# Longer runs for Q and K, score groups of two pairs, and a copy that puts K^T back in token order, in an attention-into-MoE kernel on one core

## The chip, the core and the metric

The kernel runs on one core of a Trainium2 chip. The metric is the device time of one launch in microseconds; lower is better. Before the change it takes 311.21 us (median of 3 runs, 310.49 to 313.24). Executions of one kernel differ: these three by 0.9%. Runs are compared inside one job, on the same chip, with runs of the kernel before that the job shares. A ratio below is the mean time of one kernel's fast runs over that of the other's fast runs of the same rounds, so it is not quite the ratio of the medians quoted beside it. The profile shows one execution in microseconds from its start. Its engines are PE (TensorE, matmuls), ACT (ScalarE), DVE (VectorE), POOL (GpSimd) and SP (SyncE, which here issues most transfers). PSUM is the memory that TensorE writes its results to.

## The reference

Sliding-window causal attention (8 batches, 8 heads, 576 tokens, 64 columns a head, window 64), whose output goes straight into a two-layer MoE-style product:

```python
scores = scale * np.matmul(q, k.transpose(0, 1, 3, 2))      # q, k, v: (8, 8, 576, 64)
mask = (rel >= 0) & (rel < 64)
attn = softmax(where(mask, scores, -1e9))
x = (attn @ v).transpose(0, 2, 1, 3).reshape(4608, 512)     # tokens by features
h = x @ w_in                                                # (512, 2048)
out = (h * clip(h + 3, 0, 6) / 6) @ w_out                   # (2048, 512)
```

## The kernel before

A Python planner holds an estimated clock for each engine and emits instructions in the order that its estimates give. The hardware then runs each engine's list in that order, and waits where data is missing (DVE's lines below show it).

The 4608 tokens are cut into nine steps of 512. A step T has a *first product* (x times w_in, 64 matmuls of 512 columns, eight chunks; ACT makes relu, DVE makes `gT`) and a *second product* (gT times w_out, 64 matmuls). Into the second product of step T the attention of batch T+1 is inserted at fixed places. For batches 2 to 7:

```python
def tr(t, i=i, n=n):                 # i = 0: Q, 1: K
    def fn(s):
        nc.sync.dma_start_transpose(out=QK_tiles[b % NQT][:, i * NG : (i + 1) * NG, :]..., in_=n[:]...)
        fr, land = moved(s, 655, 230)          # the plan's KB and GB/s
        ...
        return land
...
def moved(now, kb, rate):
    dma["t"] = max(dma["t"], now) + kb / rate
    land = dma["t"] + 1.9 + dma["lag"]         # lag is 0.8 once the weights are loaded
    return max(now + 0.06, dma["t"] - 5.0), land
...
# loads of Q, K: 128 tokens at a time, 64 floats (256 bytes) a run
in_=src[b, :, kb * P : kb * P + ss, :].rearrange("h s d -> s h d")
...
# first product: three PSUM tiles are shared by all chunks
hT = two_banks([("g", T, c)])                  # free again when gT of the chunk is made
nc.tensor.matmul(hT[:, j, dst : dst + w], lhsT=win16[...], rhs=xT[:, g, src : src + w], ...)
...
REST = ((4, "S", 0), (10, "S", 1), (17, "S", 2), (17, "PV", 0), (23, "S", 3), (23, "PV", 1),
        (28, "PV", 2), (33, "PV", 3))          # after which of the 64 products what is inserted
```

Q and K are loaded naturally, cast to bf16 on Pool, and transposed by DMA into one single buffer `QKT`. S is the score matmuls of a pair of heads with its exponentials on ACT and its mask on DVE, PV is P times V.

The softmax here doesn't subtract the row's maximum and nothing guards it: scores larger than these inputs give would overflow.

Of the kernel before, what the change touches and what calls it, by code (L numbers as in the profile page):

```python
# [10 lines left out]
F32 = mybir.dt.float32  # L11
# [3 lines left out]
MULT = mybir.AluOpType.mult  # L15
# [6 lines left out]
NQT = 1  # L22
NPT = 4
VGAP = 1.8
VGAP2 = 1.8
# [79 lines left out]
def kernel(  # L105
# [15 lines left out]
    assert D == 64 and NG * P == DM and WINDOW == D  # L121
    KB = (S + P - 1) // P
    SP = KB * P
    R = 9
# [71 lines left out]
    NV = NG * KB * 2 * VW  # L196
    W_ring = [runs_flat[:, i * NV : (i + 1) * NV].rearrange("p (g k h w) -> p g k h w", g=NG, k=KB, h=2) for i in range(2)]
    BL = S // D

# [20 lines left out]
    def band(t, fill):  # L220
# [24 lines left out]
        out=m64[:], in_=m64[:], pattern=[[-1, D]], compare_op=ISGE, fill=0.0, base=-1, channel_multiplier=1), "m64")  # L245
    pl.op("DVE", 26.2, 0.1, lambda s: nc.vector.tensor_copy(out=mask64[:], in_=m64[:]) and None, "mask64", deps=("m64",))
    for i, t in enumerate(W_ring):
# [24 lines left out]
    def cast_op(eng, out_ap, in_ap):  # L272
# [7 lines left out]
        "cast": lambda e, n: {"POOL": 0.18, "DVE": 0.19, "ACT": 0.18}[e] + {"POOL": 0.83e-3, "DVE": 0.45e-3, "ACT": 0.83e-3}[e] * n,  # L280
        "spread": lambda e, n: {"DVE": 0.156, "ACT": 0.165}[e] + {"DVE": 1.04e-3, "ACT": 0.83e-3}[e] * n,
        "x": lambda e, n: {"DVE": 0.156, "ACT": 0.165}[e] + {"DVE": 0.52e-3, "ACT": 0.83e-3}[e] * n,
    }

    def copy_op(kind, engs, n, ready, out_ap, in_ap, key, then=None):

        cost = {e: COST[kind](e, n) for e in engs}
        if len(cost) == 1:
            eng = engs[0]
            pl.op(eng, ready, cost[eng], cast_op(eng, out_ap, in_ap), key, then)  # L290
        else:
            pl.op(cost, ready, 0, lambda eng: cast_op(eng, out_ap, in_ap), key, then)

# [129 lines left out]
    def load_nat(b):  # L423
        for i, src in enumerate((q, k)):
# [7 lines left out]
            def tr(t, i=i, n=n):  # L432
                def fn(s):
                    nc.sync.dma_start_transpose(
                        out=QK_tiles[b % NQT][:, i * NG : (i + 1) * NG, :].rearrange("d g (k t) -> d (g k) t", t=P),
                        in_=n[:].rearrange("p g k d -> p (g k d)"),
                    )
                    fr, land = moved(s, 655, 230)
                    pl.free["SP"] = fr
                    pl.mark(("issued", b, i), s)  # L440
                    return land
                d = (("S", b - NQT, NG - 1),) if b >= NQT else ()
                if b > 2:
                    d += (("s1", b - 1),)
                pl.op("SP", t, 0.1, fn, ("tr", b, i), deps=d)
            for kb in range(KB):
                ss = min(P, S - kb * P)
                def go(s, i=i, src=src, kb=kb, ss=ss, T=T, n=n, tr=tr):
                    if kb == 0:
# [9 lines left out]
                    fr, land = moved(s, 262 * ss / P, 205)  # L459
                    def done(t):  # L460
                        T["left"] -= 1
                        if not T["left"]:
                            tr(t)
                    pl.op("POOL", land, 0.61,
# [162 lines left out]
    def kwin(b, g, i, h):  # L627

        t = QK_tiles[b % NQT]
        c = (2 * g + 1 if b < NR6 else NG + g) * SP + (i - 1) * D  # L630
        return t[:].rearrange("p a s -> p (a s)")[h * D : (h + 1) * D, c : c + P]

    def blocks(b, g):
        n = b * NG + g
        return P_ring[n % NPT][:].rearrange("p h k w -> p (h k w)")[:, 0 : 2 * S].rearrange("p (h c) -> p h c", h=2)

    def scores64(b, g):

        for i in range(2):
            pl.wait(("tr", b, i))  # L640
        QT, pT = qk(b, 0, g), blocks(b, g)
        for part in range(2):
            i0, i1 = ((0, 5), (5, BL))[part]
            st = two_banks([("exp", b, g, part)])
            for i in range(i0, i1):
                for h in range(2):
                    c = (i - i0) * D
                    nc.tensor.matmul(  # L648
                        st[:, h, c : c + D], lhsT=kwin(b, g, i, h), rhs=QT[h * D : (h + 1) * D, i * D : (i + 1) * D],
                        start=True, stop=True,  # L650
                    )
            pl.pe((0.25, 0.22)[part])
            def ex(s, st=st, i0=i0, i1=i1):
                nc.scalar.activation(  # L654
                    out=pT[:, :, i0 * D : i1 * D], in_=st[:, :, 0 : (i1 - i0) * D], func=EXP, scale=scale,
                )
            def msk(t):
                pl.op("DVE", t, 0.8, lambda s: nc.vector.tensor_tensor(  # L658
                    out=pT.rearrange("p h (i w) -> p (h i) w", w=D), in0=pT.rearrange("p h (i w) -> p (h i) w", w=D),
                    in1=mask64[:].unsqueeze(1).to_broadcast([P, 2 * BL, D]), op=MULT,  # L660
                ) and None, ("mask", b, g), deps=("mask64",))
            pl.op("ACT", pl.t + 0.1, (0.8, 0.69)[part], ex, ("exp", b, g, part), msk if part else None)
        pl.mark(("S", b, g), pl.t)

    def pv64(b, g, o):

        V, W, pT = V_ring[b % 2], W_ring[b % 2], blocks(b, g)
        for h in range(2):
# [64 lines left out]
    def xt(b, g, cell):  # L733
# [9 lines left out]
        x0 = x_at(b)  # L743
        copy_op("x", X_ENG[b][g], S, pl.t + 0.1, xT[:, g, x0 : x0 + S], tr[:, 0:S], ("x", b, g))


    def s1(T):
# [11 lines left out]
        for c in range(NCH):  # L759
# [4 lines left out]
            if c == 0:  # L764
                order.sort(key=lambda x: x[2] == NG - 1 and x[1] is parts[-1])
            for j, (dst, src, w), g in order:
                nc.tensor.matmul(  # L767
                    hT[:, j, dst : dst + w], lhsT=win16[:, g, (2 * c + j) * P : (2 * c + j + 1) * P],
                    rhs=xT[:, g, src : src + w], start=(g == 0), stop=(g == NG - 1),
                )  # L770
                pl.pe(0.216 * w / TB)
# [53 lines left out]
    def finish(T, ts, acc, c0, c1):  # L825
        u0 = T * TB + ts * P
        nst = T * 4 + ts + (c0 > 0)
        cell = {}
        def cp(s):
# [3 lines left out]
            if c0:  # L833
                nc.scalar.dma_start(out=out[u0 : u0 + P, c0:c1], in_=osb[:, c0:c1])
        def store(t):
            def fn(s):
                nc.sync.dma_start(out=out[u0 : u0 + P, c0:c1], in_=cell["o"][:, c0:c1])
                fr, land = moved(s, 262, 375)
                pl.free["SP"] = fr
                return land  # L840
            pl.op("SP", t, 0.1, fn, ("st", nst))
# [29 lines left out]
    for r in held.pop():  # L871
# [6 lines left out]
             (0, "X", 1), (0, "PV", 3), (0, "X", 2), (0, "X", 3))  # L878
    REST = ((4, "S", 0), (10, "S", 1), (17, "S", 2), (17, "PV", 0), (23, "S", 3), (23, "PV", 1),
            (28, "PV", 2), (33, "PV", 3))  # L880
    for T in range(NTB):
# [40 lines left out]
```

## Time and profile before

| | before |
|---|---|
| median, us | 311.21 (310.49 to 313.24) |
| span of the profiled run, us | 308.9 |
| TensorE busy | 96% |
| DVE, ACT, Pool busy | 52%, 51%, 38% |
| DMA packets | 153,487 |

The costliest groups of TensorE, from the page. The columns are line, engine, operation, output and inputs, form and count, then busy microseconds and mean nanoseconds of one, then idle microseconds just before them and what ended them:

```profile
L815 PE MATMUL acc<-wout,gT 128*128 128x512 bf16 (+2 forms) x559 | 129.3, 373 | 3.1 <-issue 2.2
L767 PE MATMUL ps<-xT,win 128*128 128x512 bf16 (+4 forms) x696 | 125.8, 340 | 0.5
...
L648 PE MATMUL ps<-QKT 64*128 64x64 bf16 x432 | 10.5, 191 | 1.5 <-DMA QKT<-nat 1.2
```

The means are latencies of overlapped matmuls, so 129.3 and 125.8 are not independent costs. Before all 696 recorded matmuls of the first product (L767) TensorE was idle for 0.5 us together.

### The profile page before, as it was taken

How to read it: one execution, taken by the hardware profiler on the slowest of the kernel's cores; microseconds unless marked ns; L12 is line 12 of the kernel's file. 1: busy time of each engine (PE TensorE's matmuls, PEld its weight loads, DVE VectorE, ACT ScalarE, POOL GpSimd, SP SyncE). 2: the span in 40 equal slices, each digit the busy share in tenths (PEclk: the TensorE clock that was granted, in tenths of full speed). 3: DMA queues.
4: the chain of work that ended last, by engine and by line, in shares of the span. 5: the costliest groups of instructions: out<-in, count | busy, mean ns of one | idle time of the engine just before them, and what ended most of it. 6: DMA issues, size and time to landing. Idle time of an engine off the chain costs nothing.

```text
span 308.9 us, 6664 instructions
## 1 busy us (share of the span) xinstructions
PE 296.3 (96%) x2746; PEld 153.7 (50%) x2787; DVE 161.5 (52%) x208; ACT 157.4 (51%) x199; POOL 118.1 (38%) x185
## 2 busy tenths in 40 slices
PE   8979999998999999999999999999999999999995
PEld 3544445643544454875444544454665544444443
DVE  5576675566614673377437742674276516404610
ACT  5946677465515661567156724662367246315611
POOL 3267558537824751457228522762252000000000
PEclk9999999999999999999999999999999999999999
DMA  8999999999999997999799989999990520010011
GB/s 225 255 361 388 388 324 213 268 223 222 202 191 262 252 221 152 214 232 202 168 221 260 200 165 209 258 214 164 218 188 33 118 74 0 34 70 35 0 68 70
DMA packets 153487, 58.38 MB, mean 189 GB/s; under 512 B 142064, under 2 KB 143344, under 8 KB 153456
## 3 DMA queue, kind: packets, MB, share of 16 engines
q1 hardware_dynamic: 125184, 50.80, 75.8%
q10 hardware_dynamic: 28272, 7.15, 12.3%
q8 instruction: 22, 0.36, 0.5%
q14 instruction: 9, 0.07, 0.1%
HBM read 36.70 MB, written 9.44 MB: 149 GB/s over the span
## 4 chain that ended last, share of the span: by engine, by line
PE 74%; DMA 14%; SPq 6%; POOL 4%; issue 2%; ACT 0%; ACTq 0%; POOLq 0%
PE acc L815 35%; PE ps L767 32%; DMA st<-in_v_dram 5%; DMA st<-in_moe_w_out_dram 5%; PE ps L672 3%; PE ps L648 3%; SPq L354 2%; DMA st<-in_q_dram 2%; SPq L329 2%; DMA xT<-opg 1%; SPq L412 1%; POOL V L277 1%; POOL runs L277 1%; POOL wout L277 1%; PE ps L737 0%
## 5 line engine op out<-in xcount | busy, mean ns | idle before, releaser
L779 DVE SCALAR_TENSOR_TENSOR gT<-t,ps 128x1024 bf16<-128x1024 bf16 x72 | 87.8, 1221 | 100.9 <-ACT t L776 100.9
L815 PE MATMUL acc<-wout,gT 128*128 128x512 bf16 (+2 forms) x559 | 129.3, 373 | 3.1 <-issue 2.2
L767 PE MATMUL ps<-xT,win 128*128 128x512 bf16 (+4 forms) x696 | 125.8, 340 | 0.5
L776 ACT ACTIVATE t<-ps,half 128x1024 bf16<-128x1024 f32 x72 | 80.1, 1114 | 48.9 <-PE ps L767 48.9
L767 PEld LDWEIGHTS <-win 128*128 128x128 bf16 x704 | 65.2, 98 | 59.8 <-issue 0.4
L815 PEld LDWEIGHTS <-gT 128*128 128x128 bf16 x592 | 53.6, 98 | 57.9
L832 ACT COPY osb<-acc 128x512 f32<-128x512 f32 (+2 forms) x37 | 21.3, 576 | 76.0 <-PE acc L815 75.3
L277 POOL CAST runs<-st 64x512 bf16<-64x512 f32 (+1 forms) x49 | 31.1, 635 | 65.2 <-DMA st<-in_v_dram 41.3
L277 POOL CAST nat<-st 128x512 bf16<-128x512 f32 x48 | 33.8, 716 | 20.2 <-DMA st<-in_k_dram 13.4
L654 ACT ACTIVATE pT<-ps 128x640 bf16<-128x640 f32 (+1 forms) x48 | 28.7, 650 | 11.2 <-PE ps L648 11.1
L713 DVE TENSOR_TENSOR opg<-ps,rec 128x640 bf16<-128x640 f32 x32 | 26.4, 824 | 1.1
L658 DVE TENSOR_TENSOR pT<-pT,mask 128x1152 bf16<-128x1152 bf16 x24 | 20.2, 843 | 6.9 <-ACT pT L654 6.9
L277 POOL CAST V<-st 128x512 bf16<-128x512 f32 (+1 forms) x30 | 19.3, 643 | 3.8 <-DMA st<-in_v_dram 2.2
L648 PEld LDWEIGHTS <-QKT 64*128 64x128 bf16 x432 | 7.6, 95 | 11.4 <-issue 9.7
L602 ACT ACTIVATE pT<-ps 128x768 bf16<-128x768 f32 x16 | 12.7, 834 | 0.8 <-PE ps L593 0.7
L672 PE MATMUL ps<-runs,pT 128*64 128x65 bf16 x288 | 12.4, 197 | 0.2 <-POOL runs L277 0.2
L672 PEld LDWEIGHTS <-pT 128*64 128x64 bf16 x480 | 9.6, 111 | 6.0 <-issue 4.1
L710 DVE RECIPROCAL rec<-ps 128x10 f32<-128x10 f32 x32 | 6.9, 217 | 9.8 <-PE ps L672 8.4
L648 PE MATMUL ps<-QKT 64*128 64x64 bf16 x432 | 10.5, 191 | 1.5 <-DMA QKT<-nat 1.2
L672 PE MATMUL ps<-V,pT 128*64 128x65 bf16 x192 | 11.5, 198 | 0.0
L276 ACT COPY QKT<-ps 128x1152 bf16<-128x1152 bf16 x8 | 8.9, 1129 | 4.8 <-PE ps L562 4.8
L274 DVE CAST runs<-st 128x576 bf16<-128x576 f32 x14 | 7.2, 520 | 5.8 <-DMA st<-in_q_dram 3.9
(60 smaller groups left out, 118.9 us busy)
## 6 DMA issues: line engine op xcount, KB each, us to landing
out_dram<-osb SPq DMA_DIRECT2D x35, 256.0 KB, 3.7
st<-in_q_dram SPq DMA_DIRECT2D x24, 256.0 KB, 6.0
st<-in_k_dram SPq DMA_DIRECT2D x24, 256.0 KB, 5.4
st<-in_v_dram ACTq DMA_DIRECT2D x24, 256.0 KB, 5.1
st<-in_moe_w_out_dram SPq DMA_DIRECT2D x4, 1024.0 KB, 13.1
st<-in_moe_w_in_dram SPq DMA_DIRECT2D x3, 1024.0 KB, 10.3
st<-in_q_dram SPq DMA_DIRECT2D x8, 288.0 KB, 6.7
st<-in_k_dram SPq DMA_DIRECT2D x8, 288.0 KB, 6.3
```

The source lines that it names most:

```text
L277: return lambda s: nc.gpsimd.tensor_copy(out=out_ap, in_=in_ap) and None
L602: nc.scalar.activation(out=pT[:, :, kbs[0] : kbs[0] + 2, 0:QW], in_=st[:, :, 0 : 2 * QW].rearrange("p h (k w) -> p h k w", k=2), func=EXP, ...
L648: nc.tensor.matmul(st[:, h, c : c + D], lhsT=kwin(b, g, i, h), rhs=QT[h * D : (h + 1) * D, i * D : (i + 1) * D], start=True, stop=True,)
L654: nc.scalar.activation(out=pT[:, :, i0 * D : i1 * D], in_=st[:, :, 0 : (i1 - i0) * D], func=EXP, scale=scale,)
L658: pl.op("DVE", t, 0.8, lambda s: nc.vector.tensor_tensor(out=pT.rearrange("p h (i w) -> p (h i) w", w=D), in0=pT.rearrange("p h (i w) -> p ...
L672: nc.tensor.matmul(o[odd * D : (odd + 1) * D, h, m * VW : (m + 1) * VW], lhsT=pT[:, h, i * D : (i + 1) * D], rhs=(V if i % 2 else W)[:, g, ...
L713: nc.vector.tensor_tensor(out=opg[:].rearrange("p k h d -> p h k d"), in0=ov[:, :, :, 0:D], in1=rec[:].unsqueeze(3).to_broadcast([P, 2, KB ...
L767: nc.tensor.matmul(hT[:, j, dst : dst + w], lhsT=win16[:, g, (2 * c + j) * P : (2 * c + j + 1) * P], rhs=xT[:, g, src : src + w], start=(g ...
L776: nc.scalar.activation(out=t1[:], in_=hT[:], func=RELU, bias=half[:], scale=1.0 / 6.0)
L779: nc.vector.scalar_tensor_tensor(out=gT[:, 2 * c : 2 * c + 2, :], in0=cell["t"][:], scalar=1.0, in1=hT[:], op0=MIN, op1=MULT,)
L815: nc.tensor.matmul(accs[ts][:, c0:c1], lhsT=gT[:, fc, ts * P : (ts + 1) * P], rhs=wout16[:, fc, c0:c1], start=(fc == 0), stop=(fc == NFC - 1),
L832: nc.scalar.copy(out=osb[:, c0:c1], in_=acc[:, c0:c1])
```

## The change

Its intent is to take work off the DMA, the switches and the PSUM tiles. Four consecutive tokens lie together in memory, 4 x 64 floats. If partition p takes tokens 4p to 4p+3, a run is 1 KB instead of 256 bytes. The transposed Q and K then stand in the order (token mod 4, token div 4). For Q this order is carried on: scores read Q in blocks of 4 x 16 columns, the mask and the first product follow, and the store writes every fourth row. K must be in token order for the sliding window, so five copies per batch straighten it into a tile `KN`; each goes to whichever of Pool and DVE the plan expects to finish it sooner. Scores go in groups of two pairs, in three parts of six blocks of 64 queries. Their places in the second product move later.

```diff
+LONG = (0, 1)
+KN_ENG = ("POOL", "DVE")
...
+        "kn": lambda e, n: {"DVE": 0.12, "POOL": 0.2}[e] + {"DVE": 1.2e-3, "POOL": 1.65e-3}[e] * n,
...
-                pl.op("SP", t, 0.1, fn, ("tr", b, i), deps=d)
+                pl.op("SP", t, 0.1, fn, ("tr", b, i), straighten if i else None, deps=d)
+            def straighten(t):
...
+                kd = (("S", b - 1, NG - 1), "knz")
+                copy_op("kn", KN_ENG, NG * D, t, KN[:, :, D + J * P : D + S], Kp[:, :, J * P : S], None, one, deps=kd)
+                for g in range(NG):
+                    copy_op("kn", KN_ENG, J * P, t, KN[:, g, D : D + J * P].rearrange("d (p j) -> d p j", j=J),
+                            Kp[:, g, 0 : J * P].rearrange("d (j p) -> d p j", j=J), None, one, deps=kd)
...
+                            in_=src[b, 4 * hh : 4 * hh + 4, 0 : J * P, :].rearrange("h (p j) d -> p h (j d)", j=J),
...
+        pl.wait(("tr", b, 0))
+        pl.wait(("kn", b))
...
+                if T >= NR6:
+                    i0, i1 = dst // D, (dst + w) // D
+                    xs = xs.rearrange("d (i j p) -> d j i p", j=J, p=D // J)
+                    hs = hT[:, j].rearrange("f (j i p) -> f j i p", j=J, p=D // J)[:, :, i0:i1]
...
+        rows = rows.rearrange("(p j) d -> j p d", j=J)[ts] if T >= NR6 else rows[ts * P : (ts + 1) * P]
...
-    REST = ((4, "S", 0), (10, "S", 1), (17, "S", 2), (17, "PV", 0), (23, "S", 3), (23, "PV", 1),
-            (28, "PV", 2), (33, "PV", 3))
+    REST = ((11, "S", 0), (18, "S", 1), (25, "PV", 0), (25, "PV", 1), (35, "PV", 2), (35, "PV", 3))
```

More of the change, by code (lines that the diff above doesn't have):

```diff
@@ L122 @@
     KB = (S + P - 1) // P
+    J = S // P
     SP = KB * P
@@ L197 @@
     W_ring = [runs_flat[:, i * NV : (i + 1) * NV].rearrange("p (g k h w) -> p g k h w", g=NG, k=KB, h=2) for i in range(2)]
+    KN = runs_flat[:, 2 * NV : 2 * NV + NG * (D + S)].rearrange("p (g t) -> p g t", g=NG)
     BL = S // D
@@ L245 @@
         out=m64[:], in_=m64[:], pattern=[[-1, D]], compare_op=ISGE, fill=0.0, base=-1, channel_multiplier=1), "m64")
-    pl.op("DVE", 26.2, 0.1, lambda s: nc.vector.tensor_copy(out=mask64[:], in_=m64[:]) and None, "mask64", deps=("m64",))
+    pl.op("DVE", 26.2, 0.1, lambda s: nc.vector.tensor_copy(
+        out=mask64[:].rearrange("k (j p) -> k j p", j=J), in_=m64[:].rearrange("k (p j) -> k j p", j=J)) and None, "mask64", deps=("m64",))
+    pl.op("DVE", 0.0, 0.2, lambda s: nc.vector.memset(KN[:, :, 0:D], 0.0) and None, "knz", deps=(("T", NR6 - 1, NG - 1),))
     for i, t in enumerate(W_ring):
@@ L281, with copy_op @@
         "spread": lambda e, n: {"DVE": 0.156, "ACT": 0.165}[e] + {"DVE": 1.04e-3, "ACT": 0.83e-3}[e] * n,
+        "kn": lambda e, n: {"DVE": 0.12, "POOL": 0.2}[e] + {"DVE": 1.2e-3, "POOL": 1.65e-3}[e] * n,
         "x": lambda e, n: {"DVE": 0.156, "ACT": 0.165}[e] + {"DVE": 0.52e-3, "ACT": 0.83e-3}[e] * n,
     }
-    def copy_op(kind, engs, n, ready, out_ap, in_ap, key, then=None):
+    def copy_op(kind, engs, n, ready, out_ap, in_ap, key, then=None, deps=()):
         cost = {e: COST[kind](e, n) for e in engs}
@@ L289, in copy_op @@
             eng = engs[0]
-            pl.op(eng, ready, cost[eng], cast_op(eng, out_ap, in_ap), key, then)
+            pl.op(eng, ready, cost[eng], cast_op(eng, out_ap, in_ap), key, then, deps=deps)
         else:
-            pl.op(cost, ready, 0, lambda eng: cast_op(eng, out_ap, in_ap), key, then)
+            pl.op(cost, ready, 0, lambda eng: cast_op(eng, out_ap, in_ap), key, then, deps=deps)
     def load_items():
@@ L444, in tr, with one, done, go @@
                     d += (("s1", b - 1),)
-                pl.op("SP", t, 0.1, fn, ("tr", b, i), deps=d)
-            for kb in range(KB):
+                pl.op("SP", t, 0.1, fn, ("tr", b, i), straighten if i else None, deps=d)
+            def straighten(t):
+                Kp = QK_tiles[b % NQT][:, NG : 2 * NG, :]
+                left = [NG + 1]
+                def one(t):
+                    left[0] -= 1
+                    if not left[0]:
+                        pl.mark(("kn", b), t)
+                kd = (("S", b - 1, NG - 1), "knz")
[3 more added lines that the diff above has]
+                            Kp[:, g, 0 : J * P].rearrange("d (j p) -> d p j", j=J), None, one, deps=kd)
+            def done(t, T=T, tr=tr):
+                T["left"] -= 1
+                if not T["left"]:
+                    tr(t)
+            if i in LONG:
+                for hh in range(2):
+                    def go(s, i=i, src=src, hh=hh, T=T, n=n, done=done):
+                        if hh == 0:
+                            T["t"] = stage.tile([P, H, J * D], F32, name="st", tag="st")
+                        nc.sync.dma_start(
+                            out=T["t"][:, 4 * hh : 4 * hh + 4, :],
+                            in_=src[b, 4 * hh : 4 * hh + 4, 0 : J * P, :].rearrange("h (p j) d -> p h (j d)", j=J),
+                        )
+                        fr, land = moved(s, 524, 320)
+                        for g in (2 * hh, 2 * hh + 1):
+                            pl.op("POOL", land, 0.62, cast_op(
+                                "POOL", n[:, g, 0:J, :].rearrange("p j (h d) -> p h j d", h=2),
+                                T["t"][:, 2 * g : 2 * g + 2, :].rearrange("p h (j d) -> p h j d", j=J)),
+                                ("cast", b, i, g), done)
+                        return fr
+                    yield b, deps, go
+            for kb in (KB - 1,) if i in LONG else range(KB):
                 ss = min(P, S - kb * P)
-                def go(s, i=i, src=src, kb=kb, ss=ss, T=T, n=n, tr=tr):
+                def go(s, i=i, src=src, kb=kb, ss=ss, T=T, n=n, done=done):
                     if kb == 0:
@@ L459, in go @@
                     fr, land = moved(s, 262 * ss / P, 205)
-                    def done(t):
-                        T["left"] -= 1
-                        if not T["left"]:
-                            tr(t)
                     pl.op("POOL", land, 0.61,
@@ L627, in kwin @@
     def kwin(b, g, i, h):
-        t = QK_tiles[b % NQT]
-        c = (2 * g + 1 if b < NR6 else NG + g) * SP + (i - 1) * D
-        return t[:].rearrange("p a s -> p (a s)")[h * D : (h + 1) * D, c : c + P]
-    def blocks(b, g):
-        n = b * NG + g
-        return P_ring[n % NPT][:].rearrange("p h k w -> p (h k w)")[:, 0 : 2 * S].rearrange("p (h c) -> p h c", h=2)
-    def scores64(b, g):
-        for i in range(2):
-            pl.wait(("tr", b, i))
-        QT, pT = qk(b, 0, g), blocks(b, g)
-        for part in range(2):
-            i0, i1 = ((0, 5), (5, BL))[part]
-            st = two_banks([("exp", b, g, part)])
-            for i in range(i0, i1):
+        return KN[h * D : (h + 1) * D, g, i * D : i * D + P]
@@ new lines, with turned, scores64 @@
+    halves = {}
+    NB = 6
+    def turned(t, i):
+        if i == BL - 1:
+            return t[:, i * D : (i + 1) * D].rearrange("d (p j) -> d j p", j=J)
+        return t[:, 0 : J * P].rearrange("d (j p) -> d j p", j=J)[:, :, i * (D // J) : (i + 1) * (D // J)]
+    def scores64(b, gg):
+        pl.wait(("tr", b, 0))
+        pl.wait(("kn", b))
+        pT = P_ring[(b * 2 + gg) % NPT][:].rearrange("p h k w -> p (h k w)")[:, 0 : 4 * S].rearrange("p (h c) -> p h c", h=2)
+        todo = [(2 * gg + a, i) for a in range(2) for i in range(BL)]
+        for part in range(3):
+            st = two_banks([("exp", b, gg, part)])
+            for c, (g, i) in enumerate(todo[part * NB : part * NB + NB]):
@@ L646, in scores64 @@
                 for h in range(2):
-                    c = (i - i0) * D
                     nc.tensor.matmul(
-                        st[:, h, c : c + D], lhsT=kwin(b, g, i, h), rhs=QT[h * D : (h + 1) * D, i * D : (i + 1) * D],
-                        start=True, stop=True,
-                    )
-            pl.pe((0.25, 0.22)[part])
-            def ex(s, st=st, i0=i0, i1=i1):
+                        st[:, h, c * D : (c + 1) * D], lhsT=kwin(b, g, i, h),
+                        rhs=turned(qk(b, 0, g), i)[h * D : (h + 1) * D], start=True, stop=True,
+                    )
@@ L654, in ex, with msk @@
+            pl.pe(0.27)
+            def ex(s, st=st, part=part):
                 nc.scalar.activation(
-                    out=pT[:, :, i0 * D : i1 * D], in_=st[:, :, 0 : (i1 - i0) * D], func=EXP, scale=scale,
+                    out=pT[:, :, part * NB * D : (part + 1) * NB * D], in_=st[:, :, 0 : NB * D], func=EXP, scale=scale,
                 )
-            def msk(t):
+            def msk(t, a=part - 1):
+                P_half = pT[:, :, a * S : (a + 1) * S].rearrange("p h (i w) -> p h i w", w=D)
@@ L658, in msk @@
                 pl.op("DVE", t, 0.8, lambda s: nc.vector.tensor_tensor(
-                    out=pT.rearrange("p h (i w) -> p (h i) w", w=D), in0=pT.rearrange("p h (i w) -> p (h i) w", w=D),
-                    in1=mask64[:].unsqueeze(1).to_broadcast([P, 2 * BL, D]), op=MULT,
-                ) and None, ("mask", b, g), deps=("mask64",))
-            pl.op("ACT", pl.t + 0.1, (0.8, 0.69)[part], ex, ("exp", b, g, part), msk if part else None)
-        pl.mark(("S", b, g), pl.t)
+                    out=P_half, in0=P_half,
@@ L665, in pv64 @@
+                    in1=mask64[:].unsqueeze(1).unsqueeze(1).to_broadcast([P, 2, BL, D]), op=MULT,
+                ) and None, ("mask", b, 2 * gg + a), deps=("mask64",))
+            pl.op("ACT", pl.t + 0.1, 0.82, ex, ("exp", b, gg, part), msk if part else None)
+        for a in range(2):
+            halves[b, 2 * gg + a] = pT[:, :, a * S : (a + 1) * S]
+            pl.mark(("S", b, 2 * gg + a), pl.t)
     def pv64(b, g, o):
-        V, W, pT = V_ring[b % 2], W_ring[b % 2], blocks(b, g)
+        V, W, pT = V_ring[b % 2], W_ring[b % 2], halves.pop((b, g))
@@ L743, in xt, with one @@
         x0 = x_at(b)
-        copy_op("x", X_ENG[b][g], S, pl.t + 0.1, xT[:, g, x0 : x0 + S], tr[:, 0:S], ("x", b, g))
+        if b == 0:
+            copy_op("x", X_ENG[b][g], S, pl.t + 0.1, xT[:, g, x0 : x0 + S], tr[:, 0:S], ("x", b, g))
+            return
+        c = NR6 * TB - b * S
+        left = [2]
+        def one(t):
+            left[0] -= 1
+            if not left[0]:
+                pl.mark(("x", b, g), t)
+        copy_op("x", X_ENG[b][g], c, pl.t + 0.1, xT[:, g, x0 : x0 + c], tr[:, 0:c], None, one)
+        copy_op("x", X_ENG[b][g], S - c, pl.t + 0.1,
+                xT[:, g, x0 + c : x0 + S].rearrange("d (i j p) -> d i j p", j=J, p=D // J),
+                tr[:, c:S].rearrange("d (i p j) -> d i j p", j=J, p=D // J), None, one)
     def s1(T):
@@ L766, in s1 @@
             for j, (dst, src, w), g in order:
+                xs, hs = xT[:, g, src : src + w], hT[:, j, dst : dst + w]
+                if T >= NR6:
+                    i0, i1 = dst // D, (dst + w) // D
+                    xs = xs.rearrange("d (i j p) -> d j i p", j=J, p=D // J)
+                    hs = hT[:, j].rearrange("f (j i p) -> f j i p", j=J, p=D // J)[:, :, i0:i1]
                 nc.tensor.matmul(
-                    hT[:, j, dst : dst + w], lhsT=win16[:, g, (2 * c + j) * P : (2 * c + j + 1) * P],
-                    rhs=xT[:, g, src : src + w], start=(g == 0), stop=(g == NG - 1),
+                    hs, lhsT=win16[:, g, (2 * c + j) * P : (2 * c + j + 1) * P],
+                    rhs=xs, start=(g == 0), stop=(g == NG - 1),
                 )
@@ L825, in finish @@
     def finish(T, ts, acc, c0, c1):
-        u0 = T * TB + ts * P
+        rows = out[T * TB : (T + 1) * TB]
+        rows = rows.rearrange("(p j) d -> j p d", j=J)[ts] if T >= NR6 else rows[ts * P : (ts + 1) * P]
         nst = T * 4 + ts + (c0 > 0)
@@ L833, in cp @@
             if c0:
-                nc.scalar.dma_start(out=out[u0 : u0 + P, c0:c1], in_=osb[:, c0:c1])
+                nc.scalar.dma_start(out=rows[:, c0:c1], in_=osb[:, c0:c1])
         def store(t):
             def fn(s):
-                nc.sync.dma_start(out=out[u0 : u0 + P, c0:c1], in_=cell["o"][:, c0:c1])
+                nc.sync.dma_start(out=rows[:, c0:c1], in_=cell["o"][:, c0:c1])
                 fr, land = moved(s, 262, 375)
```

## The prediction

> **What bounds the kernel now.** I read the page's first parts, then the chain that ended last, then TensorE's own waits, then one steady batch in order of time. The page first:
>
> ```profile
> PE 296.3 (96%) x2746; PEld 153.7 (50%) x2787; DVE 161.5 (52%) x208; ACT 157.4 (51%) x199; POOL 118.1 (38%) x185
> ...
> DMA  8999999999999997999799989999990520010011
> ...
> DMA packets 153487, 58.38 MB, mean 189 GB/s; under 512 B 142064, under 2 KB 143344, under 8 KB 153456
> ```
>
> The DMA row is full for three quarters of the span and nearly every packet is under 512 B, which invites the reading "DMA-bound". TensorE at 96% contradicts it. The chain decides; this is the stretch of the second MoE product that carries batch 3's attention:
>
> ```profile
> 106.53 0.86 PE acc L815 x4
> 107.39 0.37 PE ps L648 x18
> 107.76 1.40 PE acc L815 x6
> ...
> 111.14 0.37 PE ps L648 x18
> 111.51 0.44 PE ps L672 x20
> 111.95 1.18 PE acc L815 x5
> 113.14 0.15 issue
> ...
> 124.20 0.82 PE ps L767 x8
> ```
>
> It is TensorE after TensorE: scores (L648), P times V (L672) and MoE products (L815, L767), no transfer and no other engine. From 90 us on the only other pieces are short "issue" ones. What TensorE waited for, in the whole run:
>
> ```profile
> PE acc L815 <- issue: 2.2, 14, 0.2
> PE ps L850 <- DVE idle L202: 1.3, 1, 1.3
> PE ps L648 <- DMA QKT<-nat: 1.2, 1, 1.2
> PE ps L737 <- DVE opg L713: 1.1, 2, 0.6
> ```
>
> One transfer wait, 1.2 us: the scores of batch 2 start at 75.17 because the transposed K of that batch lands then. So the shortening of Q and K loads has 1.2 us to remove; everything else that DMA does is already beside TensorE.
>
> One steady step, from 106.5 to 124.2, takes 17.67 us. 64 products of 512 columns at 215.7 ns are 13.80; 4 x 0.37 of scores and 4 x 0.44 of P times V are 3.24. What is left, 0.63 us, goes to six switches from MoE work to attention and back, 0.10 each; three show as "issue" of 0.15 to 0.16.
>
> **The Trainium skill.** "TensorE: Matmul & The Clock Gate", section "Wait — 56ns, not 53.3ns?", gives 215.7 ns from start to start at 512 columns. The trace agrees: the first MoE product of this step runs from 92.28 to 106.36, 14.08 us for 64, or 220 ns with its beginning. There is nothing to win inside the products.
>
> "SBUF — State Buffer", section "Door 1: The DMA port swizzle", has a note that reads at full rate need at least two hits in each 16-byte line, and that scattered PSUM patterns slow matmuls. The new moving operands run 16 bf16 (32 bytes) before they jump, whole lines, the odd tail block steps 8 bytes, two hits a line, and the PSUM output is written in runs of 16 floats. By that page neither the scores nor the MoE products slow down. No matmul of the kernel before reads like this, so the trace can't confirm it.
>
> "DMA: Bandwidth & Descriptors", section "Specifications", puts the line-rate minimum at 512 B. The trace agrees in kind: the stretch of the 1024-KB weight loads reaches 388 GB/s in the page's GB/s row, the stretches of 256-byte runs show 150 to 270 under the same full DMA row. So 1-KB runs will be much cheaper for the DMA.
>
> "GPSIMD Engine Reference", section "Performance pitfalls for Q7 kernels", charges about 2.9 cycles an element when the read step is over 8 bytes. The straightening copy reads with a step of 256 bytes. 512 elements at 2.9 cycles and 1.2 GHz are about 1.2 us, an estimate from that page; the change's own cost table plans 1.04 on Pool and 0.73 on DVE. Nothing in the trace has this pattern on either engine.
>
> **The change, part by part.**
>
> Loads: per batch Q and K are 2 x 8 heads x 576 tokens = 9,216 runs of 256 bytes; now they are 2 x (1,024 runs of 1 KB + 512 of 256 bytes for the last 64 tokens) = 3,072. DMA packets should fall by about 6 x 6,144 = 37,000, and SP, which spends 1.07 us on each such issue (the median over 24), gets some of that back. On the path: only batch 2. Its Q and K loads are issued from 47.35 to 59.8; at the planned 320 instead of 205 GB/s they end about 3.5 us sooner, and so do its transposes.
>
> Straightening: a new serial link, K landed, then five copies (256 + 4 x 512 columns), then scores. Planned work is 0.43 + 4 x 0.73 = 3.35 us on DVE alone, about 2 us shared with Pool. The room: K's transpose of batch 3 is issued at 96.0 and lands in at most 7.2 us, 103.2, against scores at 107.32, so 4.1 us. The other batches have 4 to 5. The scores move from the 4th to the 11th product, 7 x 0.216 = 1.5 us later, so the room becomes about 5.6 and the link fits. For batch 2 the 3.5 us gained and the 1.5 of the later slot cover the copy, so the 1.2 us wait should go.
>
> What the copies do to DVE is the real cost. In the first MoE product DVE works in lockstep:
>
> ```profile
> 100.80 1.22 DVE L779 SCALAR_TENSOR_TENSOR gT<-t,ps 128x1024 bf16<-128x1024 bf16 x1 [0.50 <-ACT t L776]
> 102.53 1.22 DVE L779 SCALAR_TENSOR_TENSOR gT<-t,ps 128x1024 bf16<-128x1024 bf16 x1 [0.51 <-ACT t L776]
> 104.26 1.22 DVE L779 SCALAR_TENSOR_TENSOR gT<-t,ps 128x1024 bf16<-128x1024 bf16 x1 [0.50 <-ACT t L776]
> ```
>
> A chunk every 1.73 us, 1.22 of it busy. Copies for K land about 10.5 us into the product and fall among its last chunks. Two or three of them, 1.9 us, push one gT to about 1.3 us late if DVE also waits for the landing in program order. With three PSUM tiles a chunk must free its tile before the third next begins: the gT of 102.53 ends at 103.75, chunk 7 starts 12.1 us after 92.3, at 104.4, so 0.65 us of slack. Worst case 0.7 us of TensorE per batch in batches 3 to 7, 3.5 us; if the copies mostly go to Pool (8.45 us busy of the 14.1 between 92.2 and 106.3, so it has room) nothing.
>
> Groups of two pairs: 8 interruptions at six places become 6 at four. Two switches saved, 2 x 0.10 x 6 batches = 1.2 us. Three exponentials of 768 columns at 0.834 (the row of L602, the same size) replace four of mean 0.650: 2.50 for 2.60 us, nothing on the path. Against it: three score tiles in one go hold all three PSUM tiles, and the second group comes 1.5 us after the first ends; its third tile and P times V may wait 0.1 to 0.2 us per batch, about 1 us in all.
>
> Order kept to the store: same matmuls, same columns, store rows still 2 KB. Batch 1's x copies are split in two, four more copies of about 0.3 us, before the first product of step 1 but hidden behind it, since its last group comes last. 0 to 0.3 us.
>
> Sum: -1.2 (batch 2), -0.4 (the other short waits for V and the issue slots around it), -1.2 (switches), +1.0 (PSUM tiles), +0 to 3.5 (DVE), taken as +0.7: about -1.1. So 311.2 becomes 310.1.
>
> **Rivals.** (1) DMA was the bound in hiding, and freeing it saves 2% or more. For: the full DMA row. Against: TensorE's waits add up to 1.2 us for DMA. It would have to be under 305; I see no 6 us to take from. (2) The straightened K comes too late, or its copies block gT: TensorE waits in each of five or six batches. For: DVE is strictly in order, and the plan's landing times may be earlier than the real 7 to 10 us. Against: room of 5.6 us, and the change moves the slots to 11 and 18 for it. At 1 to 2 us a batch this gives 315 to 322. (3) Strided moving operands do slow the products. Seven steps of 13.8 us of first products are 97 us; 5% is 5 us, 316, and half rate would be beyond 400. Against: whole lines, by the page above.
>
> **Range and chances.** The kernel is at its TensorE time within about 3 us that could go, so gains are capped at some 4 us: low end 306.5. The losses have a longer tail, rivals 2 and 3: high end 315.5. Faster by over 2% (under 305.0) 4%; within 2% 84%; slower (over 317.4) 12%.
>
> **What would show it.** Right: TensorE's busy time unchanged within 1 us, no wait for QKT by batch 2's scores, packets down to some 117,000, steps of 31.2 to 31.5 us from one first product to the next, idle time of L767 still under 1 us. Wrong: a wait of L648 on the straightening copies, L767 waiting for gT, or a mean of L767 or L648 that has grown (rows now 340 and 191 ns). If the time falls under 306, my reading that nothing but TensorE bounds the steady state is wrong.

## The result and the profile after

The changed kernel takes 326.20 us (median of 4, 325.18 to 329.19), against 310.94 for the kernel before (4 runs). The ratio is 1.049, 95% interval 1.040 to 1.058: slower. Executions over 1.5% slower than the fastest of the same kernel are left out of the means. The profiled run is the slowest of the four (329.19 us, span 327.5). The same rows of the page that the prediction showed:

```profile
PE 296.9 (91%) x2752; PEld 154.3 (47%) x2787; DVE 169.9 (52%) x223; ACT 155.1 (47%) x190; POOL 138.8 (42%) x202
...
PEclk9999999996999999999999799999999999999998
DMA  8999989999069976998599849994990270020011
...
DMA packets 116239, 58.38 MB, mean 178 GB/s; under 512 B 92528, under 2 KB 106096, under 8 KB 116208
...
PE 46%; DMA 30%; DVE 7%; SPq 5%; POOL 4%; issue 3%; ACT 3%; POOLq 0%; ACTq 0%
```

Packets fell by 37,248, the sparse digits in the DMA row show that the DMA now has free time in each step, and TensorE's busy time is the same within 0.6 us. So the change did to the DMA what it set out to do, and TensorE has hardly more work. The last row is the chain by engine: TensorE's part is down to 46% (74% before), and DMA with DVE is 37%. The row of granted clock, full in the kernel before, has a 6 and a 7. TensorE's own waits say what it stood for:

```profile
PE ps L826 <- DVE gT L838: 15.6, 6, 7.3
PE ps L599 <- DVE runs L280: 2.4, 5, 0.8
PE acc L874 <- issue: 2.3, 14, 0.2
```

L826 is the first product (L767 before). It waited for `gT` six times, once in each step that prepares one of batches 2 to 7. The wait for QKT by the scores, 1.2 us before, is gone; the second row (L599) belongs to the start, where batches 0 and 1 are loaded as before. Why gT was late stands in DVE's order of work; first the step of batch 2, then (from the same view, another window) that of batch 3:

```profile
63.10 1.22 DVE L838 SCALAR_TENSOR_TENSOR gT<-t,ps 128x1024 bf16<-128x1024 bf16 x1 [2.70 <-ACT t L835]
64.82 1.22 DVE L838 SCALAR_TENSOR_TENSOR gT<-t,ps 128x1024 bf16<-128x1024 bf16 x1 [0.50 <-ACT t L835]
72.86 2.11 DVE L280 COPY runs<-QKT 128x256 bf16<-128x256 bf16 x3 [6.82 <-DMA QKT<-nat]
74.90 3.47 DVE L838 SCALAR_TENSOR_TENSOR gT<-t,ps 128x1024 bf16<-128x1024 bf16 x3
...
108.17 1.22 DVE L838 SCALAR_TENSOR_TENSOR gT<-t,ps 128x1024 bf16<-128x1024 bf16 x1 [0.51 <-ACT t L835]
111.18 1.31 DVE L280 COPY runs<-QKT 128x512 bf16<-128x512 bf16 x2 [1.79 <-DMA QKT<-nat]
112.42 3.47 DVE L838 SCALAR_TENSOR_TENSOR gT<-t,ps 128x1024 bf16<-128x1024 bf16 x3
```

The columns are start, duration, what it is, and in brackets the idle time before it and what ended it. The copies (`runs<-QKT`; `KN` lives in the old `runs` buffer) stand after the second gT in batch 2 and after the fourth in batches 3 to 7. Of the 30 copies 17 went to Pool; the 13 on DVE, two or three a batch, are enough to hold it. DVE idles 6.82 us in front of them, because K's transpose hasn't landed, and three finished relu tiles queue up behind: the gT's that follow come out back to back, 3.47 us for three. The gT's themselves are no slower, 1,218 ns each for 1,221 before. Meanwhile all three PSUM tiles are full, and TensorE stops:

```profile
60.02 8.80 PE L826 MATMUL ps<-xT,win 128*128 128x512 bf16 x39
76.16 4.16 PE L826 MATMUL ps<-xT,win 128*128 128x512 bf16 x12 [7.34 <-DVE gT L838]
```

After 39 matmuls it stands for 7.34 us. The 12 that follow take 4.16 us; twelve in a row take 2.75 in the kernel before. That is the clock. Two stretches after a stop (columns: window and its length, then busy time of PE, PEld, DVE, ACT and POOL, then granted clock, DMA share, which can exceed 1 in this view, and GB/s):

```profile
76.20:80.40 4.20, 4.20 (x14) 1.56 (x14) 2.17 (x2) 0.91 (x1) 3.83 (x7) 0.66 1.13 298
80.40:99.90 19.50, 19.02 (x225) 9.68 (x227) 10.87 (x15) 8.42 (x12) 8.85 (x14) 1.00 0.41 77
...
180.50:186.00 5.50, 5.28 (x17) 2.15 (x18) 3.40 (x3) 1.11 (x1) 5.04 (x8) 0.69 1.12 301
```

At 0.66 for 4.2 us some 1.4 us are lost, at 0.69 for 5.5 us some 1.7.

Where the time came from follows from the starts of the first products in TensorE's order of work. The step lengths from one first product to the next:

| the step that prepares batch | 2 | 3 | 4 | 5 | 6 | 7 | sum |
|---|---|---|---|---|---|---|---|
| before, us | 33.16 | 31.76 | 31.65 | 31.49 | 31.49 | 31.65 | 191.20 |
| after, us | 39.89 | 32.90 | 32.67 | 35.63 | 32.84 | 33.23 | 207.16 |
| longer by | 6.73 | 1.14 | 1.02 | 4.14 | 1.35 | 1.58 | 15.96 |
| wait for gT after | 7.34 | 1.51 | 1.24 | 2.73 | 0.82 | 1.90 | 15.54 |

The spans differ by 18.6 us: 15.96 in these six steps, 0.90 before the first of them (60.02 for 59.12), and 1.74 behind the last, where this run, the slowest of its four, had a mean clock of 0.86 in its last 9.5 us (1.00 in the kernel before). Batch 5's excess over its wait is about the lowered clock. The six steps also add up: 15.5 us of waits and about 3.1 of lowered clock, less the 2.7 us that the change gains without its part for K (e3 below), are 15.9.

Why do the copies stand where they stand? The plan gives the transposes of Q and K 2 x 655 KB at 230 GB/s, 5.7 us, and 1.9 + 0.8: it expects K about 8.4 us after the transposes start, which in batches 3 to 7 the plan does with the first product. K really landed 72.86 - 60.02 = 12.84 us into the first product for batch 2, 11.27 for batch 3 (111.18 - 99.91), 11.12 for batch 4 and 12.49 for batch 5. Before the change the same wrong estimate was harmless: the only reader of K was TensorE, 15 us into the step (107.32 - 92.28), and only batch 2 lost 1.2 us.

### The profile page after: what moved, and what is told of

The parts are those of the page before. It is cut to its first block, busy times and chain, and to the rows that moved or that the text cites. A ratio compares the mean times of both kernels' runs of the same rounds, so it can differ in the third digit from the quotient of the medians.

```text
span 327.5 us, 6643 instructions
## 1 busy us (share of the span) xinstructions
PE 296.9 (91%) x2752; PEld 154.3 (47%) x2787; DVE 169.9 (52%) x223; ACT 155.1 (47%) x190; POOL 138.8 (42%) x202
## 4 chain that ended last, share of the span: by engine, by line
PE 46%; DMA 30%; DVE 7%; SPq 5%; POOL 4%; issue 3%; ACT 3%; POOLq 0%; ACTq 0%
PE acc L874 28%; DMA QKT<-nat 16%; PE ps L826 14%; DMA st<-in_v_dram 8%; DMA st<-in_moe_w_out_dram 5%; DVE runs L280 3%; SPq L361 2%; PE ps L714 2%; ACT pT L693 2%; DVE gT L838 2%; PE ps L687 2%; POOL V L283 2%; SPq L336 1%; SPq L419 1%; POOL runs L283 1%
## 5 line engine op out<-in xcount | busy, mean ns | idle before, releaser
L826 PE MATMUL ps<-xT,win 128*128 128x512 bf16 (+4 forms) x701 | 129.2, 344 | 16.2 <-DVE gT L838 15.6
L838 DVE SCALAR_TENSOR_TENSOR gT<-t,ps 128x1024 bf16<-128x1024 bf16 x72 | 86.7, 1218 | 91.3 <-ACT t L835 91.3
L826 PEld LDWEIGHTS <-win 128*128 128x128 bf16 x704 | 65.7, 98 | 78.0 <-issue 20.2
L874 PEld LDWEIGHTS <-gT 128*128 128x128 bf16 x592 | 54.9, 98 | 61.7 <-issue 2.1
L283 POOL CAST nat<-st 128x512 bf16<-128x512 f32 x48 | 35.2, 770 | 3.2 <-DMA st<-in_q_dram 1.7
L693 ACT ACTIVATE pT<-ps 128x768 bf16<-128x768 f32 x36 | 26.9, 835 | 10.2 <-PE ps L687 10.2
L698 DVE TENSOR_TENSOR pT<-pT,mask 128x1152 bf16<-128x1152 bf16 x24 | 21.4, 907 | 15.9 <-ACT pT L693 15.9
L283 POOL COPY runs<-QKT 128x512 bf16<-128x512 bf16 (+1 forms) x17 | 18.5, 1124 | 19.8 <-DMA QKT<-nat 17.0
L280 DVE COPY runs<-QKT 128x512 bf16<-128x512 bf16 (+1 forms) x13 | 8.7, 716 | 16.5 <-DMA QKT<-nat 16.5
L639 ACT ACTIVATE pT<-ps 128x768 bf16<-128x768 f32 x16 | 12.6, 827 | 0.8 <-PE ps L630 0.7
L714 PEld LDWEIGHTS <-pT 128*64 128x64 bf16 x480 | 9.0, 111 | 5.6 <-DVE opg L755 2.5
L714 PE MATMUL ps<-runs,pT 128*64 128x65 bf16 x288 | 10.7, 197 | 0.2
L714 PE MATMUL ps<-V,pT 128*64 128x65 bf16 x192 | 10.1, 198 | 0.0
L283 POOL CAST wout<-st 128x1024 bf16<-128x1024 f32 x6 | 7.4, 1253 | 6.4 <-DMA st<-in_moe_w_out_dram 6.4
```

The costliest lines, as they stand in the source:

```text
L280: return lambda s: nc.vector.tensor_copy(out=out_ap, in_=in_ap) and None
L283: return lambda s: nc.gpsimd.tensor_copy(out=out_ap, in_=in_ap) and None
L639: nc.scalar.activation(out=pT[:, :, kbs[0] : kbs[0] + 2, 0:QW], in_=st[:, :, 0 : 2 * QW].rearrange("p h (k w) -> p h k w", k=2), func=EXP, ...
L693: nc.scalar.activation(out=pT[:, :, part * NB * D : (part + 1) * NB * D], in_=st[:, :, 0 : NB * D], func=EXP, scale=scale,)
L698: pl.op("DVE", t, 0.8, lambda s: nc.vector.tensor_tensor(out=P_half, in0=P_half, in1=mask64[:].unsqueeze(1).unsqueeze(1).to_broadcast([P, ...
L714: nc.tensor.matmul(o[odd * D : (odd + 1) * D, h, m * VW : (m + 1) * VW], lhsT=pT[:, h, i * D : (i + 1) * D], rhs=(V if i % 2 else W)[:, g, ...
```

## The experiments

The theory, A: the straightening copies stand in DVE's program order ahead of gT's that have nothing to do with them; DVE waits there for K. Rivals: B, the added serial link between K and the scores costs, on whatever engine; C, the copies' own work on DVE costs; D, the turned operands or the strided stores slow TensorE or the DMA. Eight kernels ran, all correct (no e5 or e6 is on record). Medians are beside the before of the same job (312.23 us in the first, 311.17 in the second, 11 runs each).

### e1: copies on Pool alone

```diff
-KN_ENG = ("POOL", "DVE")
+KN_ENG = ("POOL",)
```

> The straightening copies all go to Pool; nothing else changes. Theory A (the copies stand in DVE's program order ahead of gT products, DVE waits there for K's landing, gT frees no PSUM tile, TensorE stops and then runs at a lower clock): the 15.6 us that L826 waited for gT go to under 1 us, the granted clock is 1.00 throughout, and the time is 309 to 314 us, with perhaps 0 to 1.5 us a batch of scores waiting for the five serial Pool copies of 1.1 us. Rival B (the added serial link between K's landing and the scores is what costs, on whatever engine): the time stays at 322 or more and the waits move from L826 to the scores, 2 us or more in each batch, since Pool alone is slower than the two together.

318.16 us, ratio 1.018 (1.013 to 1.023). The wait for gT went as expected; the time, above 309 to 314, and the clock, 0.989 instead of 1.00, did not. The page's group of the first product, and TensorE's waits:

```profile
L826 PE MATMUL ps<-xT,win 128*128 128x512 bf16 (+4 forms) x701 | 126.0, 340 | 0.2
```

```profile
PE ps L714 <- POOL runs L283: 4.4, 5, 1.2
...
PE ps L714 <- POOL V L283: 1.4, 2, 0.9
```

The wait for gT is gone altogether (0.2 us of idle time, 340 ns as in the kernel before), so A holds for DVE, and B, which wanted 322 or more and late scores, does not: no scores waited. But P times V (L714) did, 5.8 us, for casts of V. Pool's order shows why:

```profile
72.34 4.45 POOL L283 COPY runs<-QKT 128x256 bf16<-128x256 bf16 x5 [4.36 <-DMA QKT<-nat]
76.86 0.62 POOL L283 CAST runs<-st 64x512 bf16<-64x512 f32 x1
77.54 0.62 POOL L283 CAST V<-st 128x512 bf16<-128x512 f32 x1
```

Pool is in order too: it stands 4.36 us before the copies and then copies for 4.45, and the casts of V, whose consumers come next, are behind. The queue moved from one engine to the other. I had not expected this. Batch 2 pays most: 3.7 of the 5.8 us lie there, in four waits of at most 1.2 us, and the granted clock is 0.50 from 84 to 88 us and 0.66 from 88 to 92, up to 3.4 us more. Its step is 38.03 us long (33.16 before).

### e2: the plan's landing time 3 us later

```diff
-("tr", b, i), straighten if i else None, deps=d)
+("tr", b, i), (lambda t: straighten(t + 3.0)) if i else None, deps=d)
```

> Same engines and same copies as the changed kernel; only the planned landing time of K's transpose is 3 us later, so that the copies stand two gT products later in DVE's order for batch 2 and one later for the others. Theory A: batches 3 to 7 lose their waits of 0.8 to 2.7 us (K lands about 12 us into the product, the gT they now stand behind is through by then), batch 2 keeps some 3 to 5 of its 7.3 us; L826 waits 3 to 6 us in all and the time is 313 to 317 us. Rival B (the serial link): moving the copies later in the order makes the scores later, 326 us or more. Rival C (the copies' own work on DVE, some 1.3 us per batch, is the cost, not the wait): unchanged, 324 to 327.

319.57 us, ratio 1.021 (1.015 to 1.027). The places in the order changed, and with them the plan's choice of engine: 23 copies are on DVE (16.0 us of work), for 13 (8.7 us) in the changed kernel. Still 2.8 points of the 4.9% went. TensorE's waits:

```profile
PE ps L827 <- DVE gT L839: 3.7, 1, 3.7
PE ps L600 <- DVE runs L281: 2.7, 5, 0.7
PE acc L875 <- issue: 2.1, 13, 0.2
PE ps L688 <- ACT pT L694: 1.6, 3, 0.7
```

As A expected, batches 3 to 7 lost their waits for gT in the first product and batch 2 kept 3.7 us. The time is over the expected 313 to 317: 1.6 us of scores waiting for a PSUM tile (ACT's exponentials) and 1.7 us behind late gT's in other places appeared, and a mean clock of 0.94 from 60 to 90 us is worth up to 1.8. B and C, which wanted no gain, fall as the main cause, C all the more as DVE's copying nearly doubled.

### e9 and e10: the wait without the work, the work without the wait

Both start from e3 below (308.61 us: Q in long runs, K in token order, no straightening). e9 adds one copy of 16 columns of K^T per batch that nobody reads; e10 adds two full straightening copies, but of Q^T, which has landed earlier. Both stand after the fourth gT.

```diff
 e9:
+pl.op("DVE", t, 0.06, cast_op("DVE", KN[:, 0, D : D + 16], Kp[:, 0, 0:16]), None, None, deps=kd)
 e10:
+for g in range(2):
+    pl.op("DVE", t, 0.73, cast_op("DVE", KN[:, g, D : D + J * P].rearrange("d (p j) -> d p j", j=J),
+          Qp[:, g, 0 : J * P].rearrange("d (j p) -> d p j", j=J)), None, None, deps=kd)
```

> The Q-only version (308.6 us) plus one DVE copy of 16 columns per batch that reads the transposed K and that nobody needs, standing after the fourth gT product of each step: DVE's wait for the landing without the work. Theory A (the wait at the head of DVE's order): batch 2 stops TensorE for 3 to 5 us and costs about 1 us of lowered clock, batches 3 to 7 cost 0 to 0.8 us each; in all 312.5 to 317 us. Rival C (the work of the copies): 308 to 309.5, no change.

> The same place in DVE's order, but two full copies of 512 columns in the straightening pattern that read the transposed Q, which has landed about 4 us earlier: the work, 1.3 to 1.5 us per batch, without the wait. Theory A: 308 to 310.5 us, gT waits of L828 under 0.3 us a batch since the slack there is 0.65 us. Rival C (the work): 313 or more.

e9: 316.50 us, ratio 1.016 (1.010 to 1.022). e10: 309.32 us, ratio 0.992 (0.986 to 0.998). Their DVE order, first e9 in the step of batch 2, then e10 in that of batch 3:

```profile
68.15 1.22 DVE L845 SCALAR_TENSOR_TENSOR gT<-t,ps 128x1024 bf16<-128x1024 bf16 x1 [0.50 <-ACT t L842]
74.00 0.59 DVE L280 COPY runs<-QKT 128x16 bf16<-128x16 bf16 x1 [4.62 <-DMA QKT<-nat]
74.49 3.47 DVE L845 SCALAR_TENSOR_TENSOR gT<-t,ps 128x1024 bf16<-128x1024 bf16 x3
```

```profile
100.40 1.22 DVE L847 SCALAR_TENSOR_TENSOR gT<-t,ps 128x1024 bf16<-128x1024 bf16 x1 [0.51 <-ACT t L844]
101.54 1.11 DVE L280 COPY runs<-QKT 128x512 bf16<-128x512 bf16 x2
102.56 2.51 DVE L847 SCALAR_TENSOR_TENSOR gT<-t,ps 128x1024 bf16<-128x1024 bf16 x2
```

TensorE's waits for gT, e9 and then e10 (e3 has one such wait, of 0.7 us):

```profile
PE ps L833 <- DVE gT L845: 7.3, 5, 3.6
PE ps L835 <- DVE gT L847: 0.9, 1, 0.9
```

A useless copy of 16 columns costs 7.9 us (316.50 for 308.61, or 2.75 points of ratio). Sixty-four times the columns, in the same place, cost 0.7 us (0.36 points, and the intervals overlap). e3 ran in another job than these two, but the traces agree: the six steps sum to 188.47 us in e3, 195.57 in e9 and 189.15 in e10. And e10's work is no token: DVE is busy 7.5 us longer than in e3, while all copies on DVE in the changed kernel take 8.7. This is the clean test: it is the wait at the head of DVE's order, not the work. Both times lie in A's ranges; two of e9's waits in batches 3 to 7, 1.3 and 1.4 us, are longer than the 0.8 expected.

e9 is not the whole 326. Its copy stands two gT's later in batch 2, where it stops TensorE for 3.6 us and not 7.3, and no lowered clock followed (1.00 over the run). In the other batches it stands in the same place and waits less (3.7 us in all, for 8.2); that the added work on top of the wait makes this difference is my reading, and no run separates it.

### e3: Q alone in long runs, with the groups

```diff
-LONG = (0, 1)
+LONG = (0,)
```

with the scores reading K from `QKT` as before, and no straightening.

> Q in 1-KB runs and kept in its order through the MoE, groups of two pairs, K as before in token order: no straightening copies at all. Theory A: 307.5 to 311 us, no wait for gT, clock 1.00; the turned moving operand and the strided store cost nothing (mean of the first product's matmul rows within 1% of before). Rival D (reading the moving operands in runs of 16, or storing every fourth row, slows TensorE or the stores): 316 us or more, with L826 or L687 means up.

308.61 us (307.78 to 310.50, 6 runs), ratio 0.9885 (0.984 to 0.993): 1.1% less than the kernel before. That is clear of noise, but under the 2% from which this record calls a kernel faster.

```profile
L828 PE MATMUL ps<-xT,win 128*128 128x512 bf16 (+4 forms) x701 | 126.3, 340 | 0.9 <-DVE gT L840 0.7
```

The first product now reads its moving operand in runs of 16 columns and keeps the mean of 340 ns (379 for the 512-column ones alone, as before); stores of every fourth row land in 3.8 us for 3.7 and leave no wait. So D falls for the products. Its six steps are 32.30, 30.98, 31.30, 31.39, 31.36 and 31.14 us, 2.7 us less in all than before.

### e4 and e7: the groups alone, and long Q runs alone

e4 has the score groups and their new places on the kernel before (`LONG = ()`, natural order everywhere). e7 is e3 with the scores and the places of the kernel before.

> The kernel before with only the score groups of two pairs and their later places; loads, order of Q and K and stores as before. My prediction's term: two switches fewer per batch, -1.2 us, against +1 us of waits for PSUM tiles. Expected 309.5 to 311.5 us; the 1.2 us wait of batch 2's scores for K goes too, since they start 1.5 us later, so more likely below 310.9 than above. If the groups themselves are a cost: over 313.

> The fourth corner of groups by long Q runs (before 312.2, groups alone 312.25, both 308.6 in the last job): Q in 1-KB runs, score groups and their places as before. If the gain of 3.6 us is the shorter Q loads' own, this is 308 to 309.5. If it needs both (the groups save switches but make the x transposes late under the full DMA, the shorter Q loads make room for them), it is 310.5 to 312.

| | old places, pairs | groups of two pairs |
|---|---|---|
| Q in 256-byte runs | before, 1 | e4: 312.25 us, 1.000 (0.995 to 1.005) |
| Q in 1-KB runs | e7: 311.06 us, 0.9975 (0.993 to 1.002) | e3: 308.61 us, 0.9885 (0.984 to 0.993) |

Each alone is worth nothing that these rounds can tell; together they are worth 1.1%. The intervals of e7 and e3 just touch, so that it takes both is likely, not certain. e4 is above the 309.5 to 311.5 us expected of it; e7 lies where it was expected if it takes both. In e4 the step of batch 2 fell from 33.16 to 31.27 us, and most others by 0.1 to 0.5, but the next one grew to 34.37:

```profile
PE ps L826 <- DMA xT<-opg: 2.6, 3, 1.2
```

The first product waits for the transposed x of the attention, which is made later when P times V comes later (after the 35th product). In e3 no such wait is on the list. That the lighter Q loads make the room for those transposes is my reading of the pair; no run here changes the DMA load alone beside late places. e7 removed its wait for K too, and won only 1.2 us in the step of batch 2, nothing in the others. One score block there reads

```profile
106.83 0.40 PE ps L694 x18
```

for 0.37 before: the turned Q costs 0.03 us in 18 matmuls of 64 columns, 0.12 us a batch. All 20 blocks of batches 3 to 7 read 0.39 or 0.40; before, 18 of the 20 read 0.37. A small part of D is real.

### e8: Pool alone, P times V later

```diff
-(25, "PV", 0), (25, "PV", 1), (35, "PV", 2), (35, "PV", 3))
+(33, "PV", 0), (33, "PV", 1), (40, "PV", 2), (40, "PV", 3))
```

on top of e1.

> As the Pool-only run, with P times V moved from the 25th and 35th product to the 33rd and 40th. There the cost was 5.8 us of P times V waiting for V casts that stand on Pool behind copies that wait for K. If that queue on Pool is the rest of the cost, the waits for V casts shrink to 2.5 us or less (batch 2 alone) and the time falls from 318 to 312 to 316, less whatever the x transposes, now later, add (up to 1 us a step). If the rest is something else, it stays at 317 or more.

312.83 us, ratio 1.003 (0.998 to 1.008). The waits of L714 fell from 5.8 to 2.6 us, all of it in batch 2, and 1.4 us of waits for the x transposes came, as expected. So with all parts of the change in it, and the copies in an order that holds nobody up except once, the kernel is level with before. The straightening can mostly be hidden; what it bought, shorter loads of K on a DMA for which TensorE had waited 1.2 us, does not pay for it: e3, without it, is 1.5 points faster.

## Why the prediction was wrong

It said 310.1 us, 306.5 to 315.5, with 12% for a loss over 2%. Measured is 326.2.

- **That TensorE is the bound and relief of the DMA buys almost nothing: right**, as far as these runs show. The packets fell by 37,248 (predicted 37,000) and the time rose. In e8, with both loads shortened and the order mended, nothing is gained over before; shorter Q loads gained 1.1% in e3, but only with the later places. One reading of the chain was off: it passes through a transfer of 3.67 us at 90.14 (`xT<-opg`), so "from 90 us on" should have been from 94.
- **"The 1.2 us wait should go": right** as a wait, in every variant. Wrong in its working for batch 2: K was to be some 3.5 us sooner. It landed at 72.86 for 75.17, 2.3 us sooner (3.2 if both are counted from the start of the first product), and DVE then copied for 2.11 us.
- **"Two or three of them, 1.9 us, push one gT to about 1.3 us late ... Worst case 0.7 us of TensorE per batch ... taken as +0.7": the step that failed.** The mechanism was named, its size was off by over twenty times: 15.5 us of waits, and about 3 us of lowered clock with them, against +0.7 in the sum. It priced a gT that is 1.3 us late, less 0.65 us of slack. In the run DVE stood idle for K's landing 16.5 us over the six steps, 6.82 of them in batch 2, before it copied at all. Two things were mis-sized. I took the landing at 10.5 us into the product from the kernel before and assumed that the copies would be placed there. They are placed where the plan *expects* the landing, by its constants some three to four us before K lands for batches 3 to 7 and more for batch 2, and K came a little later than before (11.1 to 12.8 us). And I used batches 3 to 7 alone: batch 2, whose copies stand after the second gT, costs 7.34 us, more than a third of the loss. The kernel's own numbers (655 KB at 230 GB/s, 1.9 + 0.8 us) would have given 8.4 us against the 10 or more in the trace; I named the gap under rival 2 and did not carry it into the sum.
- **The clock was not in the sum at all.** A stop of 7.3 us is followed by 4.2 us at 0.66.
- **That the room becomes 5.6 us and the link fits: right.** No scores waited for the straightened K in the changed kernel.
- **Rival 3 (strided operands): rightly put aside for the products**, 340 ns in e3 and before; 8% longer for the 64-column scores, 0.12 us a batch, was not foreseen. One detail of its reading is not what the code does: a full 512-column product writes PSUM in one piece, and only the products split at a batch's end write in runs, of a quarter of their width.
- **Two switches saved, -1.2 us, against +1.0 for PSUM tiles:** e4 shows no net gain (312.25 for 312.23), though through x transposes (2.6 us) and not through PSUM tiles. With Q's long runs the gain of the groups appears: e3 against e7 is 0.9 points, some 2.8 us, more than the 1.2 of the switches. The difference is within what the two intervals leave open, and I have not separated it.
- **Rival 2 was the right one**, and its size too small: 315 to 322.

## What to carry to other kernels

When work is added to an in-order engine, ask what it waits for and what stands behind it, before asking how long it takes: a 16-column copy per batch that waited for a transfer cost 7.9 us in all, two full copies that did not wait cost 0.7. A schedule made from estimates is only as good as the landing times in it, and an error that is harmless while the one reader comes late turns costly when a new reader is placed by it. A full DMA row in the profile is by itself no reason to shorten transfers when the chain through the steady steps is all TensorE.

## What the Trainium skill lacked or had wrong

- "TensorE: Matmul & The Clock Gate" (Part 1, and "Why this matters for your kernels") ties the half clock to idle gaps over about 3 to 3.4 us. Here a wait of 2.73 us was followed by 5.5 us at a mean clock of 0.69, and one of 3.61 us in e9 by 4.3 us at 1.00. That the page's window of 3.4 us runs freely would allow the second, but no whole window fits into 2.73 us; nor in e1, where TensorE had no wait over 1.2 us and was busy 1.28 of the 4.00 us from 80 to 84, and the clock was 0.50 from 84 to 88. So gaps below 3 us are not safe. How busy a window must be, no run here measures.
- "DMA: Bandwidth & Descriptors" (Latency and other measured facts) gives 261 GB/s for a DMA transpose with a scattered middle dimension. The twelve transposes of 655 KB in the changed kernel, with loads under way beside them, took 7.0 to 10.6 us each from issue to landing (median 8.4), and 4.15 us of the issuing queue each (median); at the page's rate 655 KB are 2.5 us, an estimate. What a transpose costs beside other traffic stands on no page that I read, and it was the number that mattered.
- "GPSIMD Engine Reference" (Performance pitfalls for Q7 kernels) says 2.9 cycles an element for a step over 8 bytes. The strided copies of 512 columns took 1,069 ns each on Pool in e1 (mean of 24): 2.09 ns a column with all overhead, 2.5 cycles at the page's 1.2 GHz, so the built-in copy is a little better than the page's figure.
- "SBUF — State Buffer" (the note on lines in Door 1) is right for 512-column products, 379 ns with and without runs of 16. It has nothing on short matmuls, where 18 of 64 columns went from 0.37 to 0.40 us. Its remark that any non-contiguous PSUM pattern significantly slows matmuls was not borne out: the split products, which write PSUM in runs of a quarter of their width in e3, took 246 ns at 192 columns and 326 at 384, as before.
